# A key block of a later batch asked for earlier, in a fused linear-attention and MLP-mixer kernel

## The chip, the cores and the metric

One core of one Trainium2 chip. The metric is the device time of one execution in microseconds (us). In each job the kernels ran several times beside runs of the kernel before on the same chip; different jobs ran on different chips.

## The reference, cut to what matters

```python
def phi(x):                                    # elu(x) + 1
    return np.where(x > 0, x, np.exp(x) - 1.0) + 1.0
q_p, k_p = phi(q), phi(k)                      # q, k, v: (8 batches, 8 heads, 576, 64), float32
kv  = np.einsum('bhsd,bhse->bhde', k_p, v)
z   = np.sum(k_p, axis=2)
num = np.einsum('bhsd,bhde->bhse', q_p, kv)
den = np.einsum('bhsd,bhd->bhs', q_p, z)[..., None] + 1e-06
x   = num / den                                # -> (8, 576, 512)
u   = x + (relu(x^T @ w_tok1) @ w_tok2)^T      # token mixing
out = u + relu(u @ w_ch1) @ w_ch2              # channel mixing
```

## The kernel before: the parts that matter

The kernel works through the batches in blocks. While TensorE does the channel mixing of batch n (c_ps, then h_ps), the attention and token mixing of batch n+1 are put between its matmuls. Each block is a list of large pieces (`big`) and a list of (step, function): the function is called behind the piece of that number. The schedule is by hand; each engine executes its instructions in the order in which they are called.

phi is split over two engines, for halves g = 0 and 1 of the heads:

```python
def phi_exp(nm, n, j0, nj):   # ScalarE (ACT): e = exp(raw)                       L133
    ...
def phi_add(nm, n, j0, nj):   # VectorE (DVE): y = max(raw + 1, 1)                L139
    ...
def phi_end(nm, n, j0, nj):   # VectorE: kp or qp = min(e, y), two SBUF inputs    L147
    ...
def k_exp(n):
    for g in range(2):
        phi_exp("k", n, 2 * g, 2)
def nd(n, g, rs):             # TensorE: nd_ps (num and den), VectorE: x = num / den (L226, L228, L229)
    nd_mm(n, g, rs)
    nd_end(n, g, rs)
```

nd_ps has two buffers, so the matmuls of the third nd group wait until VectorE has read the first. kvbd is the copy of kv that ScalarE makes (L182) and that these matmuls read. a_ps holds the first product of the token mixing, and uT is u transposed for the channel mixing. weight_sums makes differences of blocks of w_ch2 on GpSimd.

The block of batch 1, and that of batch 2 (`n == 2`, `d == 1`):

```python
# batch 1's block
fill += [(16, lambda: qtr_dma(3)), (23, lambda: load_all(4, "qkv"))]
fill += [(s, lambda g=g: prep_k(3, g)) for g, s in ((0, 24), (1, 26))]
fill += [(29, lambda: k_exp(4))]
run(big, sorted(fill, key=lambda e: e[0]))
... (cut)
# batch 2's block, n == 2
fill = [((AT3 if n == 2 else AT)[nm], fn) for nm, fn in steps(n + 1)]   # kv at 1, nd00 at 3, nd01 at 4, ...
for g in range(2):
    fill += [(0, lambda g=g: phi_add("k", n + 2, 2 * g, 2)),
             (1 + d + g, lambda g=g: phi_end("k", n + 2, 2 * g, 2))]    # steps 2 and 3
fill += [(3 + d, lambda: load_all(n + 3, "k"))]
... (cut)
if n + 1 == FIRST:
    fill += [(4 * i, lambda i=i: weight_sums(2 * i, 2)) for i in range(3)]
```

GpSimd (POOL) makes 18 differences of blocks of w_ch2, which later blocks use.

Of the kernel before, what the change touches and what calls it, by code (L numbers as in the profile page):

```python
# [18 lines left out]
def kernel(  # L19
# [91 lines left out]
    def load(nm, n, c, gate=None):  # L111
        src_ = src[nm][n].rearrange("(j a) (p t) d -> (a p) j (t d)", a=2, t=T)
        js = slice(2 * c, 2 * c + 2)
        return after(nc.sync.dma_start(out=raw[nm, rb(n)][:, js], in_=src_[:, js]), gate)  # L114
# [36 lines left out]
    def phi(nm, n, c):  # L151
        phi_exp(nm, n, 2 * c, 2)
        phi_add(nm, n, 2 * c, 2)
        phi_end(nm, n, 2 * c, 2)
# [49 lines left out]
    def qtr_dma(n):  # L204
        for a in range(2):
            nc.sync.dma_start_transpose(
                out=qT[n % 2][:, 2 * TD * a:2 * TD * (a + 1)].rearrange("p (f s) -> p f s", s=D),
                in_=qp[half[a]].rearrange("p c t i d -> p (c t i d)"))
# [370 lines left out]
    def row_sums(n, which, k0, m):  # L579
        ks = slice(k0, k0 + m)  # L580
        a11, a12, a21, a22 = [ablock(n, i, e)[:, ks] for e in range(2) for i in range(2)]
        x_, y_, op = {1: (a21, a22, ALU.add), 2: (sb[0][:, ks], a11, ALU.subtract),
                      3: (a11, a21, ALU.subtract), 4: (a12, sb[1][:, ks], ALU.subtract)}[which]
        nc.vector.tensor_tensor(out=sb[which - 1][:, ks], in0=x_, in1=y_, op=op)  # L584
# [94 lines left out]
    def prep_k(n, g, copy=nc.scalar.copy):  # L679
        phi("k", n, g)  # L680
        vcast(n, g, copy)
# [5 lines left out]
    def load_all(n, nms):  # L687
        if n < B:
            for nm in nms:
                for g in range(2):  # L690
                    load(nm, n, g)
# [118 lines left out]
    def steps(n):  # L810

        out_ = [("kv", lambda: kv(n, range(2)))]
        if n == 1:
            puts = [nc.scalar.copy, nc.vector.tensor_copy if n == 1 else nc.scalar.copy]
            out_ += [(f"qt{c}", lambda c=c: qtr(n, c, puts[c])) for c in range(2)]
        for i, rs in enumerate(([0, 1], [2, 3], [4])):
            for g in range(2):
                out_.append((f"nd{i}{g}", lambda g=g, rs=rs: nd(n, g, rs)))
        out_.append(("mm1", lambda: mm1(n)))
        if n > 1:  # L820
            out_ += [("mm2a", lambda: mm2(n, [0, 1])), ("mm2b", lambda: mm2(n, [2, 3]))]
            if n % 2:
                out_.append(("mm2t", lambda: mm2_tails(n // 2)))
            out_ += [("uta", lambda: utr_dma(n, [0, 1])), ("utb", lambda: utr_dma(n, [2, 3]))]
            if n % 2:
                out_.append(("utt", lambda: utr_tail_dma(n // 2)))
        return out_
# [25 lines left out]
    fill = [(2, mm2_first_tail)]  # L853
# [24 lines left out]
    fill = [(s, lambda g=g: phi("k", 2, g)) for g, s in ((0, 0), (1, 2))]  # L878
    fill += [(4, lambda: vcast(2, 0)), (5, lambda: vcast(2, 1, nc.vector.tensor_copy))]
    fill += [(at1[nm], fn) for nm, fn in steps(2)]  # L880
    fill += [(s, lambda g=g: phi("q", 3, g)) for g, s in ((0, 15), (1, 16))]
    fill += [(16, lambda: qtr_dma(3)), (23, lambda: load_all(4, "qkv"))]
    fill += [(s, lambda g=g: prep_k(3, g)) for g, s in ((0, 24), (1, 26))]
    fill += [(29, lambda: k_exp(4))]
    run(big, sorted(fill, key=lambda e: e[0]))
# [5 lines left out]
    for n in range(2, FIRST):  # L891
        p, b = divmod(n, 2)
        big = m3(n) + (m3t + m4(p, [4, 5, 6, 7, 8]) if b else m4(p, [0, 1, 2, 3]))
        fill = [((AT3 if n == 2 else AT)[nm], fn) for nm, fn in steps(n + 1)]
# [14 lines left out]
    for n in range(FIRST, B - 1):  # L909
# [7 lines left out]
        fill = []  # L917
# [48 lines left out]
    fill = [(9, lambda: row_sums(n, 3, 0, KH))]  # L966
# [32 lines left out]
```

## Time and profile before

| | before |
|---|---|
| time, median of the first 3 runs | 265.47 us (264.67 to 265.48) |
| span of the profiled run | 263.1 us |
| TensorE busy | 248.5 us, 94% |
| longest wait of TensorE in mid-kernel | 6.4 us, from 89.8 us on |

The span is that of the profiled run; times of unprofiled runs are a little longer. TensorE is the bound, so only its idle time and its half-clock stretches can be won back. The lines that show them stand in the prediction; those of a timeline have start, duration, engine, line, operation. One reading is added: VectorE's two phi ends of k of batch 4, in its timeline of the kernel before (start, duration, engine, line, operation).

```profile
94.83 1.70 DVE L147 TENSOR_TENSOR kp<-e,y 128x1152 bf16<-128x1152 bf16 x1
97.89 1.37 DVE L147 TENSOR_TENSOR kp<-e,y 128x1152 bf16<-128x1152 bf16 x1
```

### The profile page before, as it was taken

The page shows a single profiled execution, that of the slowest core. Times are in us where ns is not written, and L with a number is a line of the kernel's source. Part 1 is how long each engine was busy: PE and PEld are TensorE (multiplying, and loading weights), DVE is VectorE, ACT ScalarE, POOL GpSimd, SP SyncE. Part 2 cuts the span into 40 slices and gives each one's busy share as a digit, 9 for nine tenths or more (in the row PEclk, how much of TensorE's full clock was granted, in tenths as well). Part 3 has the DMA queues.
Part 4 walks back from the last instruction along what each step waited for, and adds up shares of the span by engine and source line. Part 5 has one row for each costly group of instructions (what it writes and reads, how often), then busy time and mean ns, then how long its engine had stood idle before and what let it go on. Part 6 is the DMA issues. An engine that isn't in the chain of part 4 may idle for free.

```text
span 263.1 us, 5476 instructions
## 1 busy us (share of the span) xinstructions
PE 248.5 (94%) x2238; PEld 149.0 (57%) x2238; DVE 174.7 (66%) x323; ACT 137.5 (52%) x217; POOL 72.5 (28%) x84
## 2 busy tenths in 40 slices
PE   7889999999999639999999999999999999999994
PEld 3574465646644325445568754675478555774873
DVE  5865769866967099855876389878974364942543
ACT  4756763397580076833675457646755255127400
POOL 9660200110011999911001510043002700070000
PEclk9999999999999959999999999999999999999999
DMA  7999999999059990079956994459443340427034
GB/s 254 254 203 274 382 199 391 243 256 411 32 121 187 411 353 20 0 158 237 379 190 113 353 214 163 107 105 333 169 99 74 79 123 0 62 48 151 2 82 117
DMA packets 49768, 48.35 MB, mean 184 GB/s; under 512 B 30096, under 2 KB 35600, under 8 KB 49744
## 3 DMA queue, kind: packets, MB, share of 16 engines
q1 hardware_dynamic: 41568, 34.87, 43.5%
q0 software_dynamic: 7632, 12.49, 22.3%
q10 hardware_dynamic: 544, 0.66, 1.0%
q8 instruction: 17, 0.28, 0.4%
q14 instruction: 7, 0.06, 0.1%
HBM read 35.85 MB, written 9.44 MB: 172 GB/s over the span
## 4 chain that ended last, share of the span: by engine, by line
PE 78%; DMA 11%; ACT 4%; POOL 3%; SPq 1%; issue 1%; DVE 0%; POOLq 0%; ACTq 0%
PE c_ps L489 27%; PE h_ps L649 14%; PE h_ps L515 13%; DMA k_raw<-in_k_dram 7%; PE a_ps L255 6%; PE c_ps L503 4%; PE h_ps L268 4%; DMA wc<-in_moe_w_ch_dram 4%; PE nd_ps L217 3%; PE h_ps L602 3%; ACT e L133 2%; PE kv_ps L176 2%; SPq L114 1%; PE y_ps L602 1%; ACT cr L496 1%; POOL qT L719 1%
## 5 line engine op out<-in xcount | busy, mean ns | idle before, releaser
L489 PE MATMUL c_ps<-uT,wc 128*128 128x512 bf16 x384 | 92.4, 382 | 0.4 <-DMA uT<-u 0.4
L496 ACT ACTIVATE cr<-c_ps 128x512 bf16<-128x512 f32 x91 | 53.4, 598 | 47.2 <-PE c_ps L489 47.2
L489 PEld LDWEIGHTS <-wc 128*128 128x128 bf16 x384 | 36.0, 99 | 37.2 <-issue 2.6
L515 PE MATMUL h_ps<-wc,cr 128*128 128x512 bf16 x144 | 34.3, 379 | 0.1
L133 ACT ACTIVATE e<-k_raw 128x1152 bf16<-128x1152 f32 x16 | 18.3, 1166 | 17.8 <-DMA k_raw<-in_k_dram 17.8
L662 POOL TENSOR_TENSOR obuf<-obuf,q_raw 128x512 f32<-128x512 f32 x4 | 5.1, 1268 | 78.9 <-ACT vs L158 39.7
L229 DVE TENSOR_TENSOR x<-nd_ps,den 128x512 bf16<-128x512 f32 (+1 forms) x42 | 25.3, 602 | 1.5
L537 POOL DMA_DIRECT2D out_dram<-obuf x12 | 7.4, 618 | 55.5 <-DVE obuf L532 55.5
L515 PEld LDWEIGHTS <-cr 128*128 128x128 bf16 x144 | 13.6, 98 | 14.9 <-issue 0.6
L133 ACT ACTIVATE e<-q_raw 128x1152 bf16<-128x1152 f32 x16 | 18.5, 1162 | 6.7 <-DMA q_raw<-in_q_dram 6.7
L217 PE MATMUL nd_ps<-kvbd,qT 128*128 128x130 bf16 x140 | 15.5, 228 | 6.4 <-ACT kvbd L182 6.4
L217 PEld LDWEIGHTS <-qT 128*128 128x128 bf16 x140 | 11.7, 100 | 16.2 <-DMA v_raw<-in_v_dram 6.7
L660 DVE TENSOR_TENSOR obuf<-h_ps,u 128x512 f32<-128x512 f32 x16 | 11.1, 691 | 13.2 <-PE h_ps L649 12.2
L139 DVE TENSOR_SCALAR y<-k_raw 128x1152 bf16<-128x1152 f32 x16 | 13.4, 853 | 8.9 <-DMA k_raw<-in_k_dram 8.7
L584 DVE TENSOR_TENSOR v_raw<-cr 128x768 bf16<-128x768 bf16 (+1 forms) x15 | 10.3, 687 | 12.8 <-ACT cr L496 12.8
L280 DVE TENSOR_TENSOR u<-h_ps,x 128x1024 bf16<-128x1024 f32 x12 | 14.6, 1220 | 4.2 <-PE h_ps L268 4.1
L649 PE MATMUL h_ps<-k_raw,v_raw 128*128 128x256 bf16 x144 | 16.7, 273 | 0.0
L649 PEld LDWEIGHTS <-cr 128*128 128x128 bf16 x144 | 14.1, 98 | 2.9
L649 PEld LDWEIGHTS <-v_raw 128*128 128x128 bf16 x144 | 13.9, 98 | 2.8 <-issue 0.8
L147 DVE TENSOR_TENSOR kp<-e,y 128x1152 bf16<-128x1152 bf16 x16 | 13.3, 849 | 3.1 <-ACT e L133 2.9
L147 DVE TENSOR_TENSOR qp<-e,y 128x1152 bf16<-128x1152 bf16 x16 | 13.2, 826 | 2.1 <-ACT e L133 1.0
L226 DVE TENSOR_SCALAR den<-nd_ps 128x8 f32<-128x8 f32 (+1 forms) x42 | 6.8, 162 | 11.4 <-PE nd_ps L217 10.8
(133 smaller groups left out, 374.4 us busy)
## 6 DMA issues: line engine op xcount, KB each, us to landing
k_raw<-in_k_dram SPq DMA_DIRECT2D x16, 576.0 KB, 8.6
q_raw<-in_q_dram SPq DMA_DIRECT2D x16, 576.0 KB, 6.1
v_raw<-in_v_dram SPq DMA_DIRECT2D x14, 576.0 KB, 9.7
out_dram<-obuf POOLq DMA_DIRECT2D x8, 512.0 KB, 6.7
wc<-in_moe_w_ch_dram POOLq DMA_DIRECT2D x8, 384.0 KB, 10.0
out_dram<-obuf POOLq DMA_DIRECT2D x12, 256.0 KB, 5.9
out_dram<-obuf POOLq DMA_DIRECT2D x6, 128.0 KB, 5.5
cr<-in_v_dram POOLq DMA_DIRECT2D x2, 288.0 KB, 7.6
```

The lines of the kernel that those rows point to most:

```text
L133: nc.scalar.activation(out=e, in_=f, func=AF.Exp)
L139: nc.vector.tensor_scalar(out=y, in0=f, scalar1=1.0, scalar2=1.0, op0=ALU.add, op1=ALU.max)
L147: nc.vector.tensor_tensor(out=dst.transpose([0, 2, 1, 3]), in0=e.rearrange("p (i t d) -> p i t d", i=nj, t=T), in1=y.rearrange("p (i t d) ...
L217: nc.tensor.matmul(out=o[:, a], lhsT=qT[b][:, t0:t0 + 128], rhs=kvbd[b][:, c, a], start=True, stop=True)
L229: nc.vector.tensor_tensor(out=x[b][:, rs[0]:rs[0] + m, HG * D * g:HG * D * (g + 1)].rearrange("p r (h d) -> p r h d", h=HG), in0=v_[:, :, ...
L255: nc.tensor.matmul(out=ps[:, mt], lhsT=w1t[:, b, ms] if r == R else w1[:, r, ms], rhs=x[b][:, r, :], start=(r == 0), stop=(r == R))
L280: nc.vector.tensor_tensor(out=u[b][:, rs[0]:rs[0] + m], in0=ps[:, 0:m], in1=x[b][:, rs[0]:rs[0] + m], op=ALU.add)
L489: nc.tensor.matmul(out=ps, lhsT=wc1[:, kj, 128 * mc:128 * mc + 128], rhs=uT[b][:, :, kj], start=(kj == 0), stop=(kj == NDM - 1))
L496: nc.scalar.activation(out=cr[b][:, mc, :], in_=ps, func=AF.Relu)
L515: nc.tensor.matmul(out=ps, lhsT=crt[:, kc, :] if t == 8 else cr[b][:, kc, 128 * r:128 * r + 128], rhs=wc2[:, kc, :], start=(kc == 0), stop ...
L649: nc.tensor.matmul(out=live[tile_][:, j], lhsT=lhs[:, k_], rhs=rhs[:, k_], start=(first and j == 0 and k_ == 0), stop=(k_ == KH - 1), skip ...
L660: nc.vector.tensor_tensor(out=o, in0=live[tile_], in1=u[n % 2][:, d::2, HC[c]], op=ALU.add)
```

## The change

The intent is to take the load of batch 4's k out of the crowd of transfers at the end of batch 1's block and to put it where the queue is empty, so that the exponentials of k do not hold up ScalarE.

```diff
-    fill += [(16, lambda: qtr_dma(3)), (23, lambda: load_all(4, "qkv"))]
+    fill += [(6, lambda: load_all(4, "k")), (16, lambda: qtr_dma(3)), (23, lambda: load_all(4, "qv"))]
```

Each engine but SyncE has the same instructions in the same order as before; on SyncE the two loads of k stand ahead of the transposes instead of between q and v.

## The prediction

> **What bounds the kernel now.** I read the page first: the totals, then the rows of 40 slices, 6.58 us each.
>
> ```profile
> span 263.1 us, 5476 instructions
> ...
> PE   7889999999999639999999999999999999999994
> ...
> PEclk9999999999999959999999999999999999999999
> DMA  7999999999059990079956994459443340427034
> ```
>
> TensorE (PE) is busy 248.5 of 263.1 us, so the kernel is bound by its matmuls almost throughout. Between the start and the last slice there is one dent: the 6 and the 3 in slices 13 and 14, counted from 0 (85.5 to 98.7 us). In slice 14 the granted clock is halved as well. DMA is at 9 in these two slices, but at 0 in slice 10 (65.8 to 72.4 us): transfers are crowded at the dent and absent some 20 us earlier. Whatever the change can gain lies in this dent, so I ask the view of waits over 52 to 110 us who waited there.
>
> ```profile
> ACT e L133 <- DMA k_raw<-in_k_dram: 14.1, 2, 13.8
> ...
> PE nd_ps L217 <- ACT kvbd L182: 6.4, 1, 6.4
> ```
>
> The matmul nd_ps waited once, 6.4 us, for ScalarE (ACT) to write kvbd; ACT itself waited for k. The chain of waits, in order of time, joins the two:
>
> ```profile
> 84.01 9.29 DMA k_raw<-in_k_dram
> ...
> 93.39 1.16 ACT e L133
> 94.55 0.97 ACT cr L496 x2
> 95.52 0.25 ACT kvbd L182
> ...
> 96.21 0.60 PE nd_ps L217 x4
> 96.81 1.71 PE c_ps L489 x4
> 98.51 0.44 PE nd_ps L217 x4
> 98.95 0.86 PE c_ps L489 x4
> ```
>
> The matmuls do not need batch 4's k. They need kvbd of batch 3, whose matmuls kv_ps ended at 87.9. But in ACT's program order the two exponentials of k of batch 4 (called at step 29, the end of batch 1's block) stand before the first work of batch 2's block, the eviction of c_ps and the copies to kvbd. ACT's timeline shows that it was free long before:
>
> ```profile
> 77.02 1.15 ACT L158 CAST vs<-v_raw 128x1152 bf16<-128x1152 f32 x1
> 91.94 1.16 ACT L133 ACTIVATE e<-k_raw 128x1152 bf16<-128x1152 f32 x1 [13.77 <-DMA k_raw<-in_k_dram]
> ```
>
> Next, why k came so late. SyncE's timeline of issues, and the DMA columns by stretch (last three columns: granted clock, DMA share, GB/s):
>
> ```profile
> 56.57 1.92 SPq L114 DMA_DIRECT2D v_raw<-in_v_dram  x2
> 72.95 2.80 SPq L206 DMA_TRANSPOSE qT<-qp  x2
> ...
> 80.85 2.06 SPq L114 DMA_DIRECT2D q_raw<-in_q_dram  x2
> 83.01 1.42 SPq L114 DMA_DIRECT2D k_raw<-in_k_dram  x2
> ```
> ```profile
> 62.00:66.00 4.00, 4.00 (x45) 2.82 (x44) 2.21 (x7) 2.51 (x5) 0.00 (x0) 1.00 1.04 408
> 66.00:67.00 1.00, 1.00 (x22) 1.00 (x20) 0.93 (x3) 0.47 (x2) 0.00 (x0) 1.00 0.37 145
> 67.00:68.00 1.00, 1.00 (x19) 0.92 (x17) 0.93 (x4) 0.47 (x2) 0.00 (x0) 1.00 0.00 0
> 68.00:70.00 2.00, 2.00 (x12) 0.99 (x11) 1.74 (x8) 2.00 (x3) 0.00 (x0) 1.00 0.00 0
> ```
>
> k of batch 4 is issued at 83.0, behind two transposes and both halves of q, and the second half lands at 93.3. Batch 3's loads, by contrast, drain at about 66.4, and the queue then does nothing until the transposes at 73.
>
> **What the Trainium skill says.** (1) "TensorE: Matmul & The Clock Gate", Part 1 (the HAM clock gate): after about 3.4 us of idle TensorE falls to half its clock, and gets it back after a busy window as long. The trace agrees: idle from 89.81, the clock is 0.50 in every stretch that I asked for from 92.0 on, and back at 1.00 from 99.0 (0.68 between 98.5 and 99.0). (2) The same page's spec table calls ScalarE's queue strictly first in, first out. The trace agrees: kvbd's copies had their input at 87.9 and ran at 95.4, behind the exponentials. (3) "DMA: Bandwidth & Descriptors", section on queues, rings and completion order: on each DMA engine a ring's descriptors are consumed in order, so a load issued behind batch 3's on the same queue should not take its bandwidth; the page's fabric ceiling is 435 GB/s, the trace reaches 403 to 422. No run here yet shows the order. (4) "SBUF — State Buffer", section "SBUF: two separate sides": VectorE and GpSimd hold a shared port pair as an exclusive lock. The trace agrees: VectorE's add of phi (L139, 128x1152) takes 751 ns on average from 50 to 90 us, and 1445 to 1640 ns from 90 to 110 us, where GpSimd makes weight differences.
>
> **The change, part by part.** Nothing is computed that was not computed; two loads of 589,824 bytes move from step 23 to step 6 of the same block, and stay on SyncE's queue.
>
> (a) When the moved loads are issued. In SyncE's order they now stand behind batch 3's loads, whose issue ends at 56.57 + 1.92 = 58.5, and before the transposes of 72.95. They must wait until the buffer is read out: batch 2's k shares it (batches from 4 on all use buffer 0, batch 2 too). Its readers are L139 on VectorE, ending 57.10 + 0.75 = 57.85, and the exponential on ACT, ending 57.23 + 1.18 = 58.4. So the issue comes at about 58.5 to 60, with no wait worth naming.
>
> (b) When they land. 2 x 589,824 bytes at the 408 GB/s of that stretch are 2.9 us, behind what drains at 66.4: about 69.3. The exponentials can run when ACT is free, at 77.02 + 1.15 = 78.2; so k is there 9 us early, and the transposes at 72.95 still find the queue empty.
>
> (c) What this takes off the path. The exponentials run from 78.2 to 80.5 in ACT's idle time (13.77 us of it). The evictions then follow the matmuls: kv_ps ends at 87.9, the kvbd copies (0.76 us together) end before 89, and nd_ps goes at 89.8 instead of 96.21. That is **6.40 us**, all on the chain.
>
> (d) The clock. With no idle time over a microsecond there the clock should not fall. Under the half clock, from 96.21 to 98.95, TensorE did two groups of nd_ps and one of c_ps; at full clock the chain has them at 0.24, 0.86 and 0.24, together 1.34 us. They took 2.74, so **1.40 us** more.
>
> (e) What is given back. GpSimd's 18 weight differences start at 87.05 whatever ACT does, so VectorE's work for batches 3 and 4 still runs beside them. From 89.8 on VectorE owes: nd00 (0.17 + 0.20 + 0.69 with gaps, 1.15), the second phi end of k (1.37 under contention), nd01 (1.1), so nd01's PSUM is free about 3.6 us after nd00's matmuls end. TensorE, no longer slowed, comes to the fourth nd group, which needs that buffer, 3 x (0.24 + 0.86) = 3.3 us after nd00's start, 3.1 after its end. The difference is an estimated **0.5 us** of new wait, once; the later groups cost VectorE 1.05 us against TensorE's 1.10 and keep up.
>
> Sum: 6.40 + 1.40 - 0.5 = 7.3 us. The three runs of before average 265.2, which leaves **257.9 us**, 2.8% less.
>
> **Rivals.** *The moved load only moves the wait.* Batch 3's q is read by ACT at 68.4, its k at 73.9, its v at 74.9. If the DMA engines served all queued loads side by side, batch 3's last data would come when everything has drained, 69.3 instead of 66.4. v and k could stand that; q was asked for at 51.4 and takes at most 8.2 us to land, near the time at which k of batch 4 can be asked for at all. So this rival makes 0, at worst 1 us. *SyncE is held up.* Were the buffer not free before 73, the transposes would be late, and with them batch 3's nd_ps. The two reads of (a) end 14 us before that; only a reader that I overlooked would make it so, and the gain would then shrink to a few us, a time of 260 to 263. *Another wait ends last.* Just behind k in the old order stand v of batch 4 (step 15 of the next block) and uT of batch 2, for which TensorE waited 0.4 us at 84.95. Neither depends on k; the 0.4 should stay. If something unseen holds kvbd or nd_ps by 3 us or more, the clock falls again and the time is about 261. *VectorE becomes the bound of block 2.* From 100 to 105 it is busy 4.69 of 5 us. If its ops take the locked lengths more often than now, 1 to 1.5 us rather than 0.5 come back: 258.4 to 258.9. *More is gained:* with no new wait in (e), 257.4.
>
> **Range and chances.** The main terms are read off one chain and barely depend on a model; what is open is (e), 0 to 1.5 us, and the scatter of before (264.67 to 265.48). So 256.8 to 259.4 holds it 8 times in 10. Faster by over 2% means under 259.9, a gain of 5.3 us or more; that fails only if a new wait eats 2 us. I give faster 0.88, within 2% 0.11, slower 0.01: nothing was added to any engine, and a late load would have to be later than the one that it replaces.
>
> **What would show it.** Right: the issue of k at 58 to 60 us and landing before 72; ACT's exponentials near 78; no wait of nd_ps on kvbd; PEclk 9 in every slice; DMA slice 10 no longer 0; a short wait (0.3 to 0.6 us) before the fourth nd group, ended by VectorE. Wrong: the transposes of 72.95 later, a wait of ACT on q, k or v of batch 3 between 68 and 78, or a fresh idle time of TensorE over 1 us between 85 and 115.

## More of the kernel before

```python
def weight_sums(k0, m):                        # ks = slice(k0, k0 + m)
    ...
    sub(tf, b12, b11)                          # 1   L568, all six
    sub(tb[0], b12, b11)                       # 2
    sub(tb[1], b22, tf[:, ks])                 # 3   reads what 1 wrote
    sub(tb[2], b22, b12)                       # 4
    sub(tf, b22, tf[:, ks])                    # 5
    sub(tb[3], b21, tf[:, ks])                 # 6   reads what 5 wrote
```

GpSimd also issues most stores of the output; the last two ahead of this run are those of `mm4_end` for the tails of batches 0 and 1 (L544).

## The result, and the profile after

The changed kernel took 261.31 us (260.21 to 261.53, 4 runs) against 265.10 us (264.67 to 265.48, 4 runs). The ratio is 0.9849, with a 95% interval from 0.9815 to 0.9884: faster, and clear of the noise, but by 1.5% and so still within the 2% to which the prediction gave a chance of 0.11; 261.31 lies above the predicted range. All ratios here are the mean time of one kernel's fast runs over that of the other's of the same rounds, so they are not quite the ratios of the medians. In a later job the same kernel gave 261.05 us and 0.9803.

The rows of the page after, for the dent at slices 13 and 14 (6.49 us each now):

```profile
span 259.6 us, 5476 instructions
...
PE   7899999999999959999999999999999999999994
...
PEclk9999999999999989999999999999999999999999
DMA  7999999999539960189948991569252440426034
```

Slice 13 is full now, but slice 14 still has a 5, and the clock still drops there, to 8. The wait is a new one, for another engine (view of waits, 52 to 110 us):

```profile
PE nd_ps L217 <- DVE x L229: 2.9, 1, 2.9
```

The load itself did what was asked of it. SyncE issued k of batch 4 from 57.59 to 59.34 us, its second half landed at about 69.8 (11.4 us after its issue at 58.4), and ScalarE ran the two exponentials at 78.04. Batch 3's last load, with k now queued behind it, landed at about 66.6, no later than before (67.3). kvbd was written by 88.41, and the first nd group started at 89.26 without waiting. Then the chain of waits goes through VectorE:

```profile
87.38 6.00 DVE kp L147
93.38 0.09 DVE den L226
...
94.47 0.41 PE nd_ps L217 x4
94.88 1.44 PE c_ps L489 x4
96.33 0.47 PE nd_ps L217 x4
96.80 1.71 PE c_ps L489 x4
```

One phi end of k took 6.00 us instead of the 0.76 that the same instruction takes where GpSimd makes no differences. VectorE works in order, so the division of nd00 stood behind it; nd00's buffer came free at 94.4, and the third nd group, due at 91.5, waited for it. GpSimd's timeline in this stretch shows what ran meanwhile:

```profile
85.94 1.20 POOL L544 DMA_DIRECT2D out_dram<-obuf  x2 [1.39 <-DVE obuf L542]
87.16 1.16 POOL L568 TENSOR_TENSOR q_raw<-wc 128x512 f32<-128x512 bf16 x1
88.27 1.16 POOL L568 TENSOR_TENSOR k_raw<-wc 128x512 bf16<-128x512 bf16 x1
89.38 1.16 POOL L568 TENSOR_TENSOR k_raw<-wc,q_raw 128x512 bf16<-128x512 bf16 x1
90.51 1.14 POOL L568 TENSOR_TENSOR k_raw<-wc 128x512 bf16<-128x512 bf16 x1
91.61 1.15 POOL L568 TENSOR_TENSOR q_raw<-wc,q_raw 128x512 f32<-128x512 bf16 x1
92.84 1.56 POOL L568 TENSOR_TENSOR q_raw<-wc,q_raw 128x512 bf16<-128x512 bf16 x1
```

Differences 1 to 5 ran undisturbed, each starting about 0.05 us before the one ahead of it had ended. Only between 5 and 6 is there a gap: 5 ended at 91.61 + 1.15 = 92.76, and 6, which reads the result of 5, started at 92.84. VectorE's phi end finished at 93.38, 0.62 us after 92.76, a little under its own undisturbed length. So it reads as if it had been let in at that gap and no earlier. This is where the theories start.

The clock, in stretches of 1 us after the wait (third number from the end):

```profile
95.00:96.00 1.00, 1.00 (x4) 0.18 (x2) 0.93 (x4) 0.00 (x0) 1.00 (x1) 0.51 0.04 14
97.00:98.00 1.00, 1.00 (x4) 0.43 (x3) 0.93 (x4) 0.00 (x0) 1.00 (x2) 0.50 0.06 16
99.00:100.00 1.00, 1.00 (x8) 0.53 (x7) 0.78 (x4) 0.59 (x2) 1.00 (x2) 1.00 0.00 0
```

### The profile page after: what moved, and what is told of

Read it like the earlier page. It is cut to its first block, busy times and chain, and to the rows that moved or that the text cites. A ratio compares the mean times of both kernels' runs of the same rounds, so it can differ in the third digit from the quotient of the medians.

```text
span 259.6 us, 5476 instructions
## 1 busy us (share of the span) xinstructions
PE 248.9 (96%) x2238; PEld 148.8 (57%) x2238; DVE 176.4 (68%) x323; ACT 137.8 (53%) x217; POOL 72.1 (28%) x84
## 4 chain that ended last, share of the span: by engine, by line
PE 81%; DMA 8%; ACT 3%; DVE 3%; POOL 3%; issue 0%; SPq 0%; POOLq 0%; DVEq 0%; ACTq 0%
PE c_ps L489 27%; PE h_ps L515 15%; PE h_ps L649 14%; PE a_ps L255 6%; PE c_ps L503 4%; PE h_ps L268 4%; DMA k_raw<-in_k_dram 4%; DMA wc<-in_moe_w_ch_dram 4%; PE nd_ps L217 3%; PE h_ps L602 3%; DVE kp L147 2%; PE kv_ps L176 2%; ACT e L133 1%; PE y_ps L602 1%; POOL qT L719 1%; POOL cr L119 1%
## 5 line engine op out<-in xcount | busy, mean ns | idle before, releaser
L537 POOL DMA_DIRECT2D out_dram<-obuf x12 | 7.4, 618 | 52.3 <-DVE obuf L532 52.3
L147 DVE TENSOR_TENSOR kp<-e,y 128x1152 bf16<-128x1152 bf16 x16 | 17.0, 1078 | 3.4 <-ACT e L133 2.9
L217 PEld LDWEIGHTS <-qT 128*128 128x128 bf16 x140 | 11.4, 100 | 13.2 <-DVE x L229 4.1
L147 DVE TENSOR_TENSOR qp<-e,y 128x1152 bf16<-128x1152 bf16 x16 | 13.8, 861 | 2.9 <-ACT e L133 1.8
L255 PE MATMUL a_ps<-x,w 128*128 128x512 bf16 x56 | 14.4, 379 | 0.0
```

Source lines behind the costliest of these rows:

```text
L147: nc.vector.tensor_tensor(out=dst.transpose([0, 2, 1, 3]), in0=e.rearrange("p (i t d) -> p i t d", i=nj, t=T), in1=y.rearrange("p (i t d) ...
L217: nc.tensor.matmul(out=o[:, a], lhsT=qT[b][:, t0:t0 + 128], rhs=kvbd[b][:, c, a], start=True, stop=True)
L255: nc.tensor.matmul(out=ps[:, mt], lhsT=w1t[:, b, ms] if r == R else w1[:, r, ms], rhs=x[b][:, r, :], start=(r == 0), stop=(r == R))
```

## The experiments

Theories. **L**: the phi end was kept out of SBUF by GpSimd's run of differences. **D**, a rival: it was slowed by the loads of q, v and the next k, which land from 86 to 94 us. **W**, another: whatever is mended, the next wait takes its place. Later L splits up over what decides how long the lock-out lasts. All results in one table ("phi end" is the first of k of batch 4; "wait" is that of TensorE on nd_ps; these and the clock are those of the one profiled run of each kernel):

| kernel | median us | ratio (95%) | phi end us | wait us | mean clock |
|---|---|---|---|---|---|
| before | 265.10 | 1 | 1.70 | 6.4 | 0.986 |
| changed | 261.31 | 0.9849 (0.9815-0.9884) | 6.00 | 2.9 | 0.992 |
| again | 261.05 | 0.9803 (0.9754-0.9852) | 6.17 | 3.0 | 0.991 |
| ws_after_both | 256.66 | 0.9665 (0.9637-0.9692) | 0.76 | none | 1.000 |
| before_ws_after_both | 264.71 | 0.9969 (0.9938-0.9999) | 0.75 | 6.8 | 0.986 |
| no_dma | 261.88 | 0.9863 (0.9826-0.9899) | 6.20 | 3.1 | 0.990 |
| reorder | 256.95 | 0.9676 (0.9645-0.9708) | 1.78 | 0.3 | 1.000 |
| indep_first | 264.39 | 0.9957 (0.9929-0.9985) | 8.40 | 5.3 | 0.986 |
| ws_after_first | 257.73 | 0.9712 (0.9685-0.9739) | 0.76, second 1.49 | 0.6 | 1.000 |
| ends_late | 258.10 | 0.9727 (0.9707-0.9747) | 1.13, second 1.72 | none | 0.999 |
| k_first_late | 263.59 | 0.9928 (0.9904-0.9951) | 1.71, add before it 5.13 | 2.1 and 1.5 | 0.990 |
| no_stores | 256.83 | 0.9645 (0.9603-0.9688) | 1.71 | none | 0.998 |
| mid_ask | 264.97 | 0.9948 (0.9894-1.0002) | 5.08 | 5.8 | 0.987 |
| memset_ahead | 257.46 | 0.9684 (0.9574-0.9795) | 0.76 | 0.3 | 1.000 |
| mid_no_stores | 260.18 | 0.9771 (0.9706-0.9836) | 1.42 | 2.2 | 1.000 |
| mid_memset | 258.61 | 0.9712 (0.9667-0.9758) | 0.75, second 1.71 | 1.5 | 1.000 |

Every kernel gave the reference's result. The last three of the list had one round only (memset_ahead, mid_no_stores, mid_memset: 2 runs each).

**1. ws_after_both: the run of differences behind the phi ends.**

```diff
-        sub(tf, b12, b11)
+        after(sub(tf, b12, b11), live["end", "k", 4, 1] if k0 == 0 else None)   # waits for the second phi end
-            fill += [(4 * i, ...weight_sums(2 * i, 2)) for i in range(3)]
+            fill += [(s, ...weight_sums(2 * i, 2)) for i, s in enumerate((4, 8, 12))]
```

> The change, with GpSimd's first weight difference made to wait for the second phi end of k of batch 4 on VectorE; nothing else moves. Theory L (GpSimd's run of differences locks VectorE out of SBUF for 5 of them): the phi end that took 6.00 us falls to about 0.76, no wait of nd_ps on x (2.9 us before), no fall of the clock, and the time is 257.3 to 258.2. Rival D (the phi end is slowed by the loads that now land from 86 to 94 us, not by GpSimd): it still takes 5 to 6 us and the time stays at 260.5 to 261.8. Rival W (the wait only moves on): the phi end is short, but another wait of over 1 us shows between 85 and 115 and the time is over 259.5.

```profile
87.71 0.76 DVE L147 TENSOR_TENSOR kp<-e,y 128x1152 bf16<-128x1152 bf16 x1
91.07 0.75 DVE L147 TENSOR_TENSOR kp<-e,y 128x1152 bf16<-128x1152 bf16 x1
```

Both phi ends take their undisturbed length, nd_ps never waits, the clock stays up, and the time is 256.66 us, a little better than L expected. The loads were still there: from 89 to 93 us the DMA share was 1.03. That speaks against D and W. This kernel beats both the kernel before and the changed one.

**2. before_ws_after_both: the same gate in the kernel before,** as a control.

> Control: the same gate on GpSimd in the kernel before, k loaded late. Theory L: the 6.4 us wait on k and the half clock stay, VectorE's adds and ends of k of batch 4 fall to 0.75 us each, and the time is 264.5 to 265.6, within 0.3% of before: delaying GpSimd has no worth by itself. If the gate itself gains 1 us or more here, a part of what the gated change gains is not due to the lock-out in the changed kernel.

264.71 us, ratio 0.9969: the gate is worth about 0.3% by itself (0.8 us by the ratio, 1.0 by the medians), hardly outside the noise. The shorter phi ends bought next to nothing behind a wait of 6.8 us on kvbd. Since 1 us is the mark that the text set, up to that much of what the gate gains in experiment 1 may not be due to the lock-out; experiment 4 gets the same gain without delaying GpSimd's run.

**3. no_dma: q and v of batch 4 asked for together with k.**

```diff
-    fill += [(6, ...load_all(4, "k")), (16, ...qtr_dma(3)), (23, ...load_all(4, "qv"))]
+    fill += [(6, ...load_all(4, "kqv")), (16, ...qtr_dma(3))]
-        fill += [(3 + d, ...load_all(n + 3, "k"))]
+        fill += [(11 if d else 3, ...load_all(n + 3, "k"))]
```

> The change, with q and v of batch 4 asked for together with its k at step 6, and k of batch 5 asked for at step 11 of the next block, so that next to nothing is loaded from 84 to 94 us; GpSimd as it is. Theory L: the phi end of k still takes about 6.0 us, with it the wait of 2.9 us, and the time is 260.2 to 261.8. Rival D: the phi end takes under 2 us and the time falls to 257.5 to 258.5.

The edit did only half of what it was for: SyncE had nothing else to do and issued k of batch 5 at 86.8 all the same, so loads ran until about 92. But the last stretch was quiet, and the phi end (from 87.61) lasted until 93.81 nevertheless. VectorE's timeline, then the stretch:

```profile
87.61 6.20 DVE L147 TENSOR_TENSOR kp<-e,y 128x1152 bf16<-128x1152 bf16 x1
```
```profile
92.00:94.00 2.00, 0.00 (x0) 0.00 (x0) 1.97 (x3) 0.48 (x1) 1.92 (x3) 1.00 0.16 64
```

261.88 us. Together with the first experiment, D has fallen.

**4. reorder: the pair that depends on each other comes first.** The second difference now reads what the first wrote.

```diff
         sub(tf, b12, b11)
-        sub(tb[0], b12, b11)
         sub(tb[1], b22, tf[:, ks])
+        sub(tb[0], b12, b11)
         sub(tb[2], b22, b12)
```

> The change, with GpSimd's differences in another order: the second one now reads what the first wrote (before, the first such pair were the fifth and sixth). Theory L1 (VectorE gets the port only where one difference has to wait for the one before): the phi end of k is let in after the first difference and takes about 1.6 us instead of 6.0; the time is 257.5 to 259.5, depending on whether the second phi end is then locked out. Theory L2 (which pair it is has nothing to do with it; the run is held for a fixed number of differences or a fixed time): still 5 to 6 us, 260.2 to 261.8.

VectorE's phi end, and GpSimd's first two differences:

```profile
87.16 1.78 DVE L147 TENSOR_TENSOR kp<-e,y 128x1152 bf16<-128x1152 bf16 x1
```
```profile
87.14 1.17 POOL L568 TENSOR_TENSOR q_raw<-wc 128x512 f32<-128x512 bf16 x1
88.39 1.57 POOL L568 TENSOR_TENSOR k_raw<-wc,q_raw 128x512 bf16<-128x512 bf16 x1
```

The gap is now between 1 and 2 (88.31 to 88.39), and the phi end finishes at 88.94, 0.63 us after 88.31. 256.95 us, below the expected range: the same gain as by the gate, from the order of two lines. L1 holds here.

**5. indep_first: the dose.** Six differences that do not depend on each other (tb[0] and tb[2] of all three slices) come first, so that the first one to wait for its predecessor is the eighth.

```diff
+        for s_ in ([slice(0, 2), slice(2, 4), slice(4, 6)] if k0 == 0 else []):
+            ...  sub(tb[0][:, s_], c12, c11);  sub(tb[2][:, s_], c22, c12)
         sub(tf, b12, b11)
-        sub(tb[0], b12, b11)
         sub(tb[1], b22, tf[:, ks])
-        sub(tb[2], b22, b12)
```

> Dose. The change, with six differences that do not depend on each other put first in GpSimd's run, so that the first one that has to wait for its predecessor's result is the eighth instead of the sixth; the sum of the work is the same. Theory L1 (VectorE stays locked out until a difference has to wait for the one just before it): the phi end of k takes about 6.0 + 2 x 1.12 = 8.2 us, the wait of nd_ps grows from 2.9 to about 5.1, and the time is 262.8 to 264.5. Theory L2 (locked out for a fixed number of differences or a fixed time of 5 to 6 us): 6.0 us and 260.2 to 261.8. If VectorE is let in after the running difference: under 2 us and 257 to 258.

```profile
87.33 8.40 DVE L147 TENSOR_TENSOR kp<-e,y 128x1152 bf16<-128x1152 bf16 x1
```
```profile
93.97 1.14 POOL L568 TENSOR_TENSOR q_raw<-wc 128x512 f32<-128x512 bf16 x1
95.19 1.56 POOL L568 TENSOR_TENSOR k_raw<-wc,q_raw 128x512 bf16<-128x512 bf16 x1
```

8.40 us against 8.2 expected, ending at 95.73, again 0.62 us after the seventh difference (95.11). 264.39 us: nearly all of the gain is gone. Only GpSimd's order differs from the changed kernel.

**6. ws_after_first: the run gated on the first phi end only** (the edit of experiment 1 with half 0 and steps 3, 8, 12).

> The change, with GpSimd's first difference made to wait for the first phi end of k of batch 4, not the second; so the run begins near 88.2 us, without stores issued just before it, and the second phi end asks near 90.5, in the third difference. Theory L1: the first takes 0.76, the second is locked out until the fifth difference ends, near 93.8, and takes 3.5 to 4 us; nd_ps waits 2 to 3 us; the time is 259.3 to 261. If the lock-out needs the stores that GpSimd issues just before its run: 1.2 to 1.7 us and 256.5 to 257.3.

L1 missed here. The second phi end asked at 91.04, during the third difference, and was let in right behind it: 1.49 us, and 257.73 us. What differs is that GpSimd had paused for 1.1 us between its stores and the run.

**7. ends_late: both phi ends behind the nd groups.**

```diff
-                     (1 + d + g, lambda g=g: phi_end("k", n + 2, 2 * g, 2))]
+                     (9 if d else 1 + g, lambda g=g: phi_end("k", n + 2, 2 * g, 2))]
```

> The change, with both phi ends of k of batch 4 on VectorE moved from between the nd groups to behind them (step 9); GpSimd as it is. Theory L, path: nothing that TensorE waits for stands behind the phi ends any more, so no wait of nd_ps on x over 0.5 us, no fall of the clock, and the time is 256.5 to 257.8, however long the phi ends take. Theory L1 on their length: the first asks near 96, after a run of differences that nothing interrupted, and is let in only where the twelfth has to wait for the eleventh, near 99.6, so it takes 3 to 4 us; if it is let in after the running difference, 1.2 to 1.7 us.

The path part holds: nd_ps no longer waits on VectorE. But VectorE is late afterwards, and a token-mixing matmul of the tails waits 1.4 us on it, so the time is 258.10 us, above the expected range. L1 on the length misses again: asking at 95.87, after the gap between 5 and 6, the first took 1.13 us: it was let in behind the running difference, though the run had not been disturbed.

**8. k_first_late: the kernel before, but with k ahead of q at step 23.**

```diff
-    fill += [(16, ...qtr_dma(3)), (23, ...load_all(4, "qkv"))]
+    fill += [(16, ...qtr_dma(3)), (23, ...load_all(4, "kqv"))]
```

> The kernel before, with k of batch 4 still asked for at step 23 but ahead of q. Its halves should land near 86 and 88 us. Theory L1: one of VectorE's two adds or the first phi end falls into GpSimd's run and is locked out until about 92.7, as in the changed kernel; the time is 260.3 to 262.5, so asking at step 6 gains nothing over asking first at step 23. Without a lock-out the late k would cost about 1 to 1.5 us over a clean path: 258 to 258.8.

The lock-out came as expected, on an add this time: it asked at 89.02, took 5.13 us and ended 0.62 us after difference 5. But the time, 263.59 us, missed the range: k still landed late enough to hold kvbd up by 2.1 us, and the two losses add up. So asking at step 6 was worth about 2 us over asking first at step 23 (2.1 by the ratios, 2.3 by the medians, of different jobs), not nothing as the text had it.

**9. no_stores: nothing of GpSimd's directly ahead of the run.** In every long lock-out so far two stores of GpSimd stood directly ahead of the run. Here SyncE issues them, and the first difference waits for VectorE's second add, so that the run starts at the same place.

```diff
-        put = nc.sync if last else nc.gpsimd
+        put = nc.sync if last or (p, t) == (0, 8) else nc.gpsimd
-        sub(tf, b12, b11)
+        after(sub(tf, b12, b11), live["add", "k", 4, 1] if k0 == 0 else None)
```

> What makes the lock-out so long: the change, with the two stores that GpSimd issues just ahead of its run issued by SyncE, and the first difference made to wait for VectorE's second add of k of batch 4, so that the run still begins near 87.1, just ahead of the first phi end, but with nothing of GpSimd's in front of it. H-A (whoever asks during the first difference of a run is kept out until a difference has to wait for the one just before): the phi end still takes about 6 us and the time is 260 to 262. H-B (the long lock-out needs the stores issued just ahead): 1.2 to 1.8 us and 256.5 to 257.8.

GpSimd's first difference, and VectorE's phi end:

```profile
87.21 1.15 POOL L568 TENSOR_TENSOR q_raw<-wc 128x512 f32<-128x512 bf16 x1 [2.57 <-issue]
```
```profile
87.26 1.71 DVE L147 TENSOR_TENSOR kp<-e,y 128x1152 bf16<-128x1152 bf16 x1 [0.19 <-PE kv_ps L176]
```

The phi end asked 0.05 us into the first difference and was let in behind it; 256.83 us. H-A has fallen.

**10. mid_ask: the stores and the six independent differences, but VectorE asks in the middle.** indep_first with both phi ends at step 3, behind nd00.

> The order with six independent differences first (indep_first), with the stores ahead of it as they are, but both phi ends of k of batch 4 moved behind nd00, so that VectorE asks near 91, in the fourth difference. H-A: let in after the running difference, 1.2 to 1.8 us, no long wait of nd_ps, 257 to 258.5. H-B in its strict form (stores ahead hold the port for VectorE throughout the run up to the eighth difference): about 4.7 us, until 95.7, a wait of nd_ps of 3 to 4 us and 261 to 263.

```profile
90.44 5.08 DVE L147 TENSOR_TENSOR kp<-e,y 128x1152 bf16<-128x1152 bf16 x1
```
```profile
93.76 1.14 POOL L568 TENSOR_TENSOR q_raw<-wc 128x512 f32<-128x512 bf16 x1
94.98 1.56 POOL L568 TENSOR_TENSOR k_raw<-wc,q_raw 128x512 bf16<-128x512 bf16 x1
```

It ended at 95.52, again behind the seventh difference (94.90). H-B holds here. The time, 264.97 us, is above its range, because both phi ends now stood ahead of nd01 and the wait was 5.8 us, not 3 to 4.

**11. again: the changed kernel once more.**

> The changed kernel itself once more, beside the two others: ratio 0.983 to 0.988, the first phi end of k of batch 4 at 5.9 to 6.2 us. If it takes under 2 us here, the lock-out is a matter of luck and not of this kernel.

6.17 us, in the expected range: the lock-out shows in both profiled runs of this kernel, so it is not a matter of luck. The ratio, 0.9803, lies below its range; the kernel itself took 261.05 us, as in the first job, while the kernel before scattered up to 268.04 beside it.

**12. memset_ahead: is it the stores, or any work directly ahead?** As no_stores, with a memset of GpSimd's own ahead of the run.

```diff
+        after(nc.gpsimd.memset(part[2], 0.0), live["add", "k", 4, 0])       # only for k0 == 0
```

> Is it the stores, or only that the run follows other GpSimd work without a pause? As no_stores (the two stores go to SyncE), but GpSimd's run follows directly on a memset of its own, a buffer that is not in use then; the memset waits for VectorE's first add of k of batch 4, which ends near 86.3, so the run begins near 87 and the first phi end asks in its first difference. If it is the stores: the phi end takes 0.8 to 1.8 us and the time is 256.5 to 258. If any work ahead without a pause is enough: about 6 us and 260 to 262.

Inconclusive: the run began at 87.72, after the phi end had started (87.48), so the phi end met no difference.

**13 and 14. mid_no_stores and mid_memset:** mid_ask with the stores on SyncE, once with the run beginning after a pause (gated as in experiment 9), once following on the memset without a pause.

> As mid_ask (six independent differences first, both phi ends behind nd00, so VectorE asks near 90.5 to 91, in the fourth difference), but with the two stores ahead of the run issued by SyncE and the first difference made to wait for VectorE's second add of k. With stores ahead (mid_ask) the first phi end took 5.3 us. If the stores ahead, or a run without a pause ahead, are what keeps VectorE out: 1.2 to 1.8 us and 256.5 to 258.5. If the row of independent differences is enough by itself: until the eighth, 4.5 to 5.5 us and 262 to 265.5.

> As mid_no_stores, but the run follows without a pause on a memset of GpSimd's own, which waits for VectorE's first add of k (the run begins near 87.7, VectorE asks near 90.9). If only the stores do it: 1.2 to 1.8 us, 256.5 to 258.5. If any GpSimd work directly ahead does it: 4.5 to 5.5 us, 262 to 265.5.

(The 5.3 us that the first text gives for mid_ask is a slip: the trace has 5.08.) The first phi end in mid_no_stores, and in mid_memset:

```profile
91.47 1.42 DVE L147 TENSOR_TENSOR kp<-e,y 128x1152 bf16<-128x1152 bf16 x1
```
```profile
91.27 0.75 DVE L147 TENSOR_TENSOR kp<-e,y 128x1152 bf16<-128x1152 bf16 x1
```

The row of differences is the same, and so is, nearly, the place of the request: 0.03 us before the third difference ended in mid_ask and 0.08 in mid_memset, 0.35 us into the fourth in mid_no_stores. The phi end took 5.08 us with GpSimd's stores directly ahead, 1.42 without them, and 0.75 behind a memset, where the fourth difference made way instead (1.71 us for 1.15). So neither the row of independent differences nor a memset directly ahead is enough; the long lock-out came only with the stores ahead. The times lie above the expected ranges, mid_memset's by 0.1 us, because both phi ends still stand ahead of nd01 (nd_ps waits 2.2 and 1.5 us).

One thing is not separated. In all six profiled runs with a long lock-out VectorE's adds of k ran beside these stores, and one of the two issues took longer: 0.67 us (1.09 in k_first_late) against 0.54 in the kernel before, where VectorE was idle. The second store in the changed kernel, then in the kernel before:

```profile
86.47 0.67 POOL L544 DMA_DIRECT2D out_dram<-obuf  x1
```
```profile
86.49 0.54 POOL L544 DMA_DIRECT2D out_dram<-obuf  x1
```

No run has the stores directly ahead and undisturbed and a request well ahead of the first gap. Whether the stores are enough, or have to be met by an add, stays open.

## Why the prediction was wrong, point by point

- **(a), (b) issue and landing of k:** right. 57.6 to 59.3 us against 58.5 to 60, and landed at about 69.8 against 69.3, still 8 us ahead of the exponentials.
- **(c) the wait of 6.40 us on kvbd:** right. ScalarE ran the exponentials at 78.04, and nd_ps started at 89.26 without a wait. The smaller wait of 0.4 us on uT, which was to stay, was gone too. It is gone as well in before_ws_after_both, which loads k as late as the kernel before, so the change need not be its reason: uT landed 6.2 us after its issue there, and 6.8 in the kernel before.
- **(d) the clock:** right to about 0.2 us, wrong in its condition. It needed TensorE to have no idle time over a microsecond, and (e) broke that. Where it was kept, in ws_after_both, TensorE took 96.85 - 89.59 = 7.26 us from the first nd group to the first matmul of a_ps, against 104.68 - 96.21 = 8.47 us in the kernel before: 1.2 us where the text has 1.40. That the spans differ by just 6.40 + 1.40 (263.1 - 255.3 = 7.8) is partly luck: the 0.4 us on uT is gone too, and ws_after_both was 0.5 us behind already at 83 us, ahead of the dent (GpSimd's store of L537 at 83.89 against 83.38). One reading is loose: of the clock's fall after about 3.4 us of idle time the text says that the trace agrees, but its own numbers have the fall at 92.0, 2.2 us after 89.81, and the clock was back about 2.6 us after 96.21. No sum rests on it.
- **(e) what VectorE gives back: the step that failed.** Its list of what VectorE owes begins at 89.8 with nd00 and so takes the first phi end as done by then; for the second it took the 1.37 us of the trace before, and got 0.5 us. It was the first that was locked out: it asked at 87.38, in GpSimd's first difference, and held nd00 up until 93.38. The second took 0.75 us. What came back: from the first nd group to the first matmul of a_ps TensorE took 101.20 - 89.26 = 11.94 us in the changed kernel, against the 7.26 us of ws_after_both. That is 4.7 us: 2.9 of wait, and 1.8 that is mostly the half clock which the wait brought on. The spans bear it out: the first nd group started 96.21 - 89.26 = 6.95 us earlier than before, the way from there to a_ps took 11.94 - 8.47 = 3.47 us longer, and what is left, 3.5 us, is 263.1 - 259.6.

The wrong size came from a biased sample. In the kernel before, VectorE first asked at 91.88, in the fifth difference, because k came late; every lock-out that this trace could show was therefore of one instruction at most. The early part of the run, behind the stores, had never been asked into. The change moved VectorE's requests there. The rival "VectorE becomes the bound" named the right engine and the right cause, but it looked at 100 to 105 us and sized the lock-out from the same sample (1 to 1.5 us).

The rivals of SyncE held up, of shared DMA bandwidth and of a later transfer did not come true. The sign that the text named for being wrong, a fresh idle time of TensorE over 1 us between 85 and 115, is the one that showed.

What stays open is why, with GpSimd's stores directly ahead, VectorE is kept out until a difference must wait for its predecessor's result, while without them it is let in behind the running difference. The runs show that it is so; they do not show the mechanism, nor whether an add of VectorE has to meet the stores. The scatter of the changed kernel (260.21 to 261.53) goes with its mean clock, 0.997 in the shortest run and 0.990 in the longest, so part of it may be how much of the wait the clock punishes; that was not tested.

## What to carry to other kernels

Before moving work earlier, list what the newly early engine will meet there that it has never met: here the durations under contention, read from a trace in which the two engines met elsewhere, did not carry over. Where GpSimd and VectorE share a stretch, look for a single VectorE instruction of several times its usual length that ends about one usual length (here 0.62 us) after a gap in GpSimd's row; then put GpSimd's run behind a dependency, order it so that the second instruction waits for the first, or move stores from its front to another queue (tried here together with a dependency that kept the run's start in place). Each of the three turned a gain of 1.5% into one of over 3% here.

## What the Trainium skill lacked or had wrong

- "SBUF — State Buffer", sections "SBUF: two separate sides" and "Who interferes with whom": an exclusive lock, held by the winner for its whole instruction. The runs agree for most meetings (1.0 to 1.8 us instead of 0.76), but the page lacks that a row of GpSimd instructions can keep VectorE out over several: 6.00 us over five, 8.40 us over seven. It also lacks what ended it: in each long case a GpSimd instruction that had to wait for the result of the one just before it.
- No page that I read has it that stores issued by GpSimd directly ahead go with the long lock-out: 5.08 us with them, 1.42 us without, at nearly the same place of the same row.
- "TensorE: Matmul & The Clock Gate", Part 1: half clock after an idle window of about 3.4 us. Here shorter waits were enough: one of 2.9 us in the changed kernel was followed by about 3.4 us at half clock (95.0 to 98.4 us), and one of 2.1 us in k_first_late by as much (91.9 to 95.3). The length of the wait does not decide it alone: one of 2.2 us in the profiled run of mid_no_stores left the clock at 1.000. The page's advice in "Why this matters for your kernels", no gaps over about 3 us, is thus too generous for this case.
